# New due times, engine choices and filler share for a scheduled attention and two-MoE kernel

## The chip, the cores and the metric

The kernel runs on one core of a Trainium2 chip. The metric is the device time of one execution in microseconds (us); shorter is better. The engines go by the profile's names: PE (matrix products; PEld is its weight loads), DVE (VectorE), ACT (ScalarE), POOL (GpSimd), and SP, which issues the DMAs.

## What is computed

A gated linear attention over 4 batches, 8 heads, 768 steps and head size 48, and behind it two pairs of dense layers ("MoE") over all 3072 tokens, 384 wide and 2048 deep:

```python
state = alpha[t] * state + k[t] ⊗ v[t]          # per batch and head, 48x48
y[t]  = q[t] @ state
...
h = x @ w_in                                    # first pair
P = a[0] + a[1]*h + a[2]*h*h + a[3]*h*h*h
Q = 1.0 + |b[0]|*|h| + |b[1]|*h*h
x = (P / (Q + 1e-6)) @ w_out
...
h = x @ w_in2                                   # second pair
out = (h * tanh(softplus(h))) @ w_out2
```

All weights come as 64-bit floats, which the kernel takes apart with integer operations.

## The kernel before

The sequence is cut into six blocks c of 128 steps. **An attention unit** is two batches of one block; there are twelve. A unit runs through levels L = 0, 1, 2, 4, 8, 16, 32 (blocks 0 to 2) or 2 to 32 after a diagonal step (blocks 3 to 5). A level is 32 small products on PE (L476, 64 records in the trace), a masked copy of them into the tile AT (L487, L507 on DVE, or L495, L501 on ACT), and on DVE a scaling of the tiles Q and K by products of alpha (L460). The products of alpha are built by a **tree** of six halving multiplications, which runs on DVE or POOL by the string E_TREE (one letter per block; V is DVE, P is POOL, A is ACT). The next level's product on PE reads the scaled Q and K, so PE and DVE take turns within a unit. Behind the levels stand transposes (L537), an outer product (L552), the state's update (tmp, X), and the outputs (L590, L626).

**A step** of a pair is one of 16 slices of 128 hidden columns for one block. On PE it is a hidden product H, nine matmuls of 512 columns (L682), and an output product O, nine more (L731). In pair l=0 the work between H and O is, on ACT, the absolute value u (L697), a scaled copy (L705), B1*u+B0 (L703), a logarithm and an exponential (L710, L714), on POOL one multiplication (L704), and on DVE three polynomial steps (L706, L708, L715). In pair l=1 it is one activation (L719). Both pairs then split the result g into a rounded part gh (L230 on ACT or L232 on DVE) and the rest gl = g - gh (line 223 on DVE or 225 on POOL, by E_GL0 and E_GL1, one letter per block).

The twelve phases (l, c) of 16 steps follow each other as PHASES says: (0,0), (0,1), (1,0), (0,2), (1,1), (0,3), (1,2), (0,4), (1,3), (0,5), (1,4), (1,5). The buffers are few: three PSUM banks for H, four slots of z and p, three of gh and gl. So H can run only some steps ahead of O. Block c+1's attention runs beside phase (0,c), since phase (0,c+1) needs its output; the conversions of the weights (`load_w`, 32 in all) lie beside the first four phases.

**What sets the order:** nothing is scheduled at run time. Every operation is given to `Plan.add` with an engine, an assumed duration and a due time. `Plan.order` then plays the plan through: each engine that is free takes the ready operation with the earliest due time, and the order in which operations start there is the order in which they are written into each engine's queue. On the chip, a queue runs in that order; an instruction whose input is late holds all behind it. Due times come from the tables T_PH, AT_T, Q_A0, Q_V0, Q_CV and some offsets. In `Plan.order`, DVE and POOL operations marked `port` exclude each other. As long as no H has been placed, free PE time before F_END is filled with matmuls of 256 columns that nobody reads (`warm`, L775), as far as F_RATE allows.

## Time and profile before

| | us |
|---|---|
| three runs | 1011.58, 1009.32, 1011.18; median 1011.18 |
| profiled execution, its own time | 1012.22 |
| its span | 1010.4 |
| PE busy | 969.7 |
| DVE busy | 689.3 |
| ACT busy | 603.4 |
| POOL busy | 252.0 |

The profiled execution took 1.04 us more than the median, and 1.8 us of it lie outside the span. PE is in use nearly throughout, but a busy PE is not a PE at its peak: matmuls overlap, and one that waits for its turn is drawn longer. In a stretch without any wait, nine matmuls of 512 columns follow each other in 2.04 us.

### The profile page before, as it was taken

The numbers are of one execution on the slowest core, as the hardware profiler recorded it, in microseconds if no ns is written. First come the engines' busy times: TensorE is split into PE (matmuls) and PEld (weight loads), VectorE is DVE, ScalarE is ACT, GpSimd is POOL, SyncE is SP. The second block draws the span as 40 slices with busy tenths as digits, with TensorE's granted clock in tenths as the row PEclk, the third lists the DMA queues.
The fourth block names the chain that finished last, engine by engine and source line by source line (L and its number), as shares of the span: only waits on it lengthen the run. The fifth ranks groups of instructions, "written<-read, shape, count | busy, mean of one in ns | idle before, by whom it ended". The sixth has DMA issues, their size and how long they took to land.

```text
span 1010.4 us, 24622 instructions
## 1 busy us (share of the span) xinstructions
PE 969.7 (96%) x10460; PEld 783.9 (78%) x10460; DVE 689.3 (68%) x876; ACT 603.4 (60%) x994; POOL 252.0 (25%) x199
## 2 busy tenths in 40 slices
PE   7899897999999999999999899999999999999998
PEld 6776676778878878878877688878788878888886
DVE  4959999899998899845589963389941178621211
ACT  3659887799756599521487652376541288733332
POOL 2115665433301155102134221045223300000000
PEclk8989998999999999999999999999999999999999
DMA  8455656837778878659538378556365555465630
GB/s 338 147 185 188 221 203 222 285 108 245 258 250 291 281 240 268 174 178 306 163 99 296 89 244 277 142 175 234 110 210 159 144 158 153 140 212 143 180 107 32
DMA packets 75469, 198.39 MB, mean 196 GB/s; under 512 B 8160, under 2 KB 34912, under 8 KB 73824
## 3 DMA queue, kind: packets, MB, share of 16 engines
q1 hardware_dynamic: 75360, 196.82, 60.4%
q8 instruction: 82, 1.34, 0.6%
q14 instruction: 27, 0.22, 0.1%
HBM read 165.34 MB, written 31.46 MB: 195 GB/s over the span
## 4 chain that ended last, share of the span: by engine, by line
PE 66%; DVE 12%; ACT 5%; DMA 3%; issue 2%; POOL 0%; SPq 0%; ACTq 0%; POOLq 0%; DVEq 0%
PE bank L731 31%; PE bank L682 29%; PE pair L476 2%; DVE zp L715 2%; DVE qka L460 2%; PE pair L626 1%; DVE zp L706 1%; DVE zp L708 1%; DMA out_dram<-u 1%; DVE AT L507 1%; DVE gg L223 1%; ACT u L697 1%; ACT zp L710 1%; ACT zp L714 1%; ACT zp L703 1%
## 5 line engine op out<-in xcount | busy, mean ns | idle before, releaser
L731 PE MATMUL bank<-gg,wo 128*128 128x512 f32 x1728 | 432.4, 395 | 1.2 <-DVE gg L223 0.6
L731 PEld LDWEIGHTS bank<-gg,wo 128*128 128x128 f32 x1728 | 324.0, 190 | 70.9 <-DVE gg L223 1.7
L682 PE MATMUL bank<-xh,wih 128*128 128x512 f32 x576 | 231.5, 402 | 5.6 <-DVE zp L708 4.3
L682 PE MATMUL bank<-xl,wih 128*128 128x512 f32 x576 | 225.3, 391 | 0.0
L682 PE MATMUL bank<-xh,wl 128*128 128x512 f32 x576 | 225.1, 391 | 0.0
L223 DVE TENSOR_TENSOR gg<-zp,gg 128x512 fp32r<-128x512 f32 x160 | 122.0, 767 | 133.4 <-ACT gg L230 132.5
L704 POOL TENSOR_TENSOR zp<-zp,u 128x512 f32<-128x512 f32 x80 | 124.1, 1554 | 266.5 <-ACT zp L703 266.2
L719 ACT ACTIVATE zp<-bank 128x512 f32<-128x512 f32 x96 | 57.0, 596 | 206.3 <-PE bank L682 205.8
L682 PEld LDWEIGHTS bank<-xh,wih 128*128 128x128 f32 x576 | 108.7, 189 | 32.2 <-DVE zp L708 7.2
L682 PEld LDWEIGHTS bank<-xh,wl 128*128 128x128 f32 x576 | 108.6, 189 | 23.5
L682 PEld LDWEIGHTS bank<-xl,wih 128*128 128x128 f32 x576 | 108.9, 189 | 21.0
L230 ACT CAST gg<-zp 128x512 fp32r<-128x512 f32 x144 | 89.3, 621 | 38.3 <-DVE zp L715 23.9
L476 PEld LDWEIGHTS pair<-qka 48*64 48x64 f32 (+4 forms) x4160 | 60.7, 129 | 40.4 <-issue 11.2
L476 PE MATMUL pair<-qka 48*64 48x32 f32 (+4 forms) x4160 | 68.3, 215 | 17.5 <-ACT AT L501 5.5
L706 DVE SCALAR_TENSOR_TENSOR zp<-zp,sc,bank 128x512 f32<-128x512 f32 x96 | 70.6, 740 | 12.9 <-ACT zp L705 12.6
L710 ACT ACTIVATE zp<-zp,c 128x512 f32<-128x512 f32 x96 | 69.7, 729 | 10.3 <-POOL zp L704 9.8
L715 DVE SCALAR_TENSOR_TENSOR zp<-zp,sc 128x512 f32<-128x512 f32 x80 | 71.6, 901 | 6.0 <-ACT zp L714 4.7
L705 ACT ACTIVATE zp<-bank,sc 128x512 f32<-128x512 f32 x96 | 66.2, 690 | 15.2 <-PE bank L682 10.2
L708 DVE SCALAR_TENSOR_TENSOR zp<-zp,sc,bank 128x512 f32<-128x512 f32 x96 | 70.9, 743 | 4.5 <-ACT u L697 2.8
L697 ACT ACTIVATE u<-bank 128x512 f32<-128x512 f32 x96 | 57.3, 600 | 24.5 <-PE bank L682 18.3
L232 DVE CAST gg<-zp 128x512 fp32r<-128x512 f32 x48 | 22.5, 472 | 66.9 <-ACT zp L719 63.6
L460 DVE TENSOR_TENSOR qka<-qka,qk 128x1024 f32<-128x1024 f32 x44 | 58.7, 1333 | 12.1 <-PE pair L476 8.4
(148 smaller groups left out, 952.3 us busy)
## 6 DMA issues: line engine op xcount, KB each, us to landing
wo<-woD SPq DMA_DIRECT2D x160, 384.0 KB, 3.3
wl<-wlD SPq DMA_DIRECT2D x160, 192.0 KB, 2.8
qka<-in_qka_dram SPq DMA_DIRECT2D x10, 1536.0 KB, 7.7
woD<-wo SPq DMA_DIRECT2D x16, 768.0 KB, 4.8
wlD<-wl SPq DMA_DIRECT2D x16, 384.0 KB, 3.9
raw<-in_w2o_dram SPq DMA_DIRECT2D x8, 768.0 KB, 5.0
...
```

Source lines behind the costliest of these rows:

```text
L223: dve(n, due, reads, writes, lambda: nc.vector.tensor_tensor(**kw()))
L230: act(n, due, reads, writes, lambda: nc.scalar.copy(out=out(), in_=in_()), src="s")
L460: dve(W, now(), [kT[L]], [kQC, kK], lambda: nc.vector.tensor_tensor(out=QK, in0=QK, in1=Tv.unsqueeze(3).to_broadcast([P, 2, m, L]), op=ALU ...
L476: nc.tensor.matmul(bk[j][o:o + m, lo + 32 * g:lo + 32 * (g + 1)].rearrange("p (n l) -> p n l", l=l), lhsT=K[h, e * HC:e * HC + m], rhs=QC[ ...
L682: nc.tensor.matmul(bank[hb], lhsT=w[:, k * P:(k + 1) * P], rhs=x[k], start=(k == 0 and j == 0), stop=(k == KT - 1 and j == 2))
L697: act(NTOK, due, [kh, "tab"], [ku], lambda: nc.scalar.activation(u, h, AF.Abs), table="ln")
L704: pool(NTOK, due, [ku], [kz], lambda: nc.gpsimd.tensor_tensor(out=zs[r], in0=zs[r], in1=u, op=ALU.mult))
L706: dve(NTOK, due, [kh], [kp], lambda: nc.vector.scalar_tensor_tensor(out=ps[r], in0=ps[r], scalar=A2, in1=h, op0=ALU.add, op1=ALU.mult), po ...
L708: dve(NTOK, due, [kh], [kp], lambda: nc.vector.scalar_tensor_tensor(out=ps[r], in0=ps[r], scalar=A1, in1=h, op0=ALU.add, op1=ALU.mult), po ...
L710: act(NTOK, due, [], [kz], lambda: nc.scalar.activation(zs[r], zs[r], AF.Ln, bias=c_1), src="s", ptr=1, table="ln")
L715: dve(NTOK, due, [kw], [kp], lambda: nc.vector.scalar_tensor_tensor(out=ps[r], in0=ps[r], scalar=A0, in1=w(), op0=ALU.add, op1=ALU.mult), ...
L731: nc.tensor.matmul(bank[5 + k], lhsT=wos[b][:, w, k * P:(k + 1) * P], rhs=x[q], start=(f == 0 and j == 0), stop=(f == FT - 1 and j == 2))
```

## The change

Only the numbers and letters that feed the plan, the assumed cost of a POOL operation, and two new forms of the weight conversion change what is built. In the weight conversion (`load_w`), form A makes the low bits by an activation on ACT; the new form B makes them by a shift on DVE. It is used by 2 of the 32 conversions; form C is used by none. The new letter G in R_PSUM and R_MISH, which keeps g in PSUM, is used by no block, so `split_g` and `hidden` build the same operations as before.

```diff
-T0 = 86.664
+T0 = 103.104
-T_PH = (9.277, 6.654, 6.157, 5.496, 14.285, 12.303, 6.406, 21.64, 8.826, 19.033, 5.941, 6.084)
+T_PH = (9.812, 5.897, 4.97, 0.365, 23.477, 6.33, 6.522, 16.525, 12.473, 8.147, 3.464, 4.853)
...
-E_TREE = 'PPPVPP'
-E_QK = 'VVPPVP'
+E_TREE = 'PPVVVP'
+E_QK = 'VVPPPP'
...
-E_GL1 = 'VVVPVV'
+E_GL1 = 'VVVPPP'
...
-E_LW = 'PVPPPVVVVVVVVVVVVVVVVVVVVVVVVVVV'
+E_LW = 'VVPPPVVGVVVVVVVVVVVVVVVVVVVVVVVV'
...
-E_CV = 'ADAAAAAAADDAADADDDDAADDDAADDDADA'
+E_CV = 'ADAAABAAADDAADADDDBAADDDAADDDADA'
...
-E_L32 = 'AV'
-E_KC = ('AA', 'AV')
+E_L32 = 'AA'
+E_KC = ('AA', 'AA')
...
-E_XH = ('AA', 'VA')
-E_DC = 'PV'
+E_XH = ('VA', 'AA')
+E_DC = 'PP'
...
-F_END = 91.927
-F_RATE = 1325.024
+F_END = 268.634
+F_RATE = 1329.217
...
-        plan.add("POOL", 0.15 + (0.0021 if n > 2 * P else 0.00254) * n, due, reads, writes, emit, True)
+        plan.add("POOL", 0.112 + (0.00217 if n == NTOK else 0.00168) * n, due, reads, writes, emit, True)
...
+            if E_CV[nth] in "BC":
+                dve(n, due, [kr], [kz], lambda: nc.vector.tensor_scalar(
+                    out=zt.bitcast(I32), in0=lw, scalar1=29, scalar2=None, op0=ALU.logical_shift_right), fast=True)
...
+            if E_CV[nth] == "A":
+                act(n, due, [kr], [kz], lambda: nc.scalar.activation(
+                    low3, quarters[:, :, 1], AF.Identity, scale=2.0 ** -13, bias=c_f), src="s", ptr=3.6)
```

The other tables (AT_T, Q_A0, Q_V0, Q_CV, LAG, the offsets) get new values in the same manner. In the built program the lines move: L476 becomes L485, L460 L469, L507 L516, L682 L691, L731 L755, L706 L715, L708 L717, L715 L726, L704 L713, L223 L224, L225 L226. PE has the same H, O and attention products in both, and five fillers more (43 against 38). POOL takes over 32 subtractions gl of phases (1,4) and (1,5) from DVE and gives the trees of blocks 2 and 4 to it; of the weights' rounding remainders (E_LW), one goes from PE to DVE and one from DVE to POOL. Two evictions and four small copies of block 0's second unit go from DVE to ACT.

**DVE in phase (0,3)**, the eighth to tenth step. L706, L708 and L715 are the polynomial steps, gg is a subtraction gl; qka and AT belong to an attention unit of block 4. Before:

```order
L708 SCALAR_TENSOR_TENSOR zp_130<-zp_130,sc_67,bank2_123 128x512
L708 SCALAR_TENSOR_TENSOR zp_130<-zp_130,sc_67,bank3_124 128x512
L507 COPY_PREDICATED AT0_140<-cst_65,pair_122 128x256x2
L460 TENSOR_TENSOR qka0_141<-qka0_141 128x2x256x2
L223 TENSOR_TENSOR gg_131<-zp_130,gg_131 128x512
L715 SCALAR_TENSOR_TENSOR zp_130<-zp_130,sc_67 128x512 x2
L706 SCALAR_TENSOR_TENSOR zp_130<-zp_130,sc_67,bank4_125 128x512
L507 COPY_PREDICATED AT0_140<-cst_65,pair_122 128x128x4
L708 SCALAR_TENSOR_TENSOR zp_130<-zp_130,sc_67,bank4_125 128x512
L706 SCALAR_TENSOR_TENSOR zp_130<-zp_130,sc_67,bank2_123 128x512
L708 SCALAR_TENSOR_TENSOR zp_130<-zp_130,sc_67,bank2_123 128x512
L460 TENSOR_TENSOR qka0_141<-qka0_141,qk0_144 128x2x128x4
```

and now:

```order
L715 SCALAR_TENSOR_TENSOR zp_130<-zp_130,sc_67,bank3_124 128x512
L717 SCALAR_TENSOR_TENSOR zp_130<-zp_130,sc_67,bank3_124 128x512
L715 SCALAR_TENSOR_TENSOR zp_130<-zp_130,sc_67,bank4_125 128x512
L224 TENSOR_TENSOR gg_131<-zp_130,gg_131 128x512
L726 SCALAR_TENSOR_TENSOR zp_130<-zp_130,sc_67 128x512
L717 SCALAR_TENSOR_TENSOR zp_130<-zp_130,sc_67,bank4_125 128x512
L715 SCALAR_TENSOR_TENSOR zp_130<-zp_130,sc_67,bank2_123 128x512
L717 SCALAR_TENSOR_TENSOR zp_130<-zp_130,sc_67,bank2_123 128x512
L224 TENSOR_TENSOR gg_131<-zp_130,gg_131 128x512
L726 SCALAR_TENSOR_TENSOR zp_130<-zp_130,sc_67 128x512 x2
L715 SCALAR_TENSOR_TENSOR zp_130<-zp_130,sc_67,bank3_124 128x512
L224 TENSOR_TENSOR gg_131<-zp_130,gg_131 128x512
```

Both units of block 4 stood in this phase before, the second in the middle of these steps; now no attention work stands in these rows. Counted from the first to the last L715 of the phase, seven scalings L460 became three and four masked copies L507 one; they stand after the phase's last step now.

**PE just before the first H.** L652 (now L661) transposes the last output of block 0; pair products with 64x32 and 60x32 are levels of block 1's first unit, L376 and L377 (now L385, L386) parts of weight conversions. Before:

```order
L652 MATMUL bank6_127<-cst_65,u_129 128x128 x3
L652 MATMUL bank7_128<-cst_65,u_129 128x128 x3
L476 MATMUL pair_122<-qka0_141 64x32 x32
L376 MATMUL bank6_127<-f320_101,cst_65 128x384
L377 MATMUL bank6_127<-wih0_0_71,minus_70 128x384
L376 MATMUL bank7_128<-xf_105,cst_65 128x384
L377 MATMUL bank7_128<-wih0_1_72,minus_70 128x384
L476 MATMUL pair_122<-qka0_141 64x32 x32
L376 MATMUL bank6_127<-xf_105,cst_65 128x384
L377 MATMUL bank6_127<-wih0_1_72,minus_70 128x384
L682 MATMUL bank2_123<-xh_107,wih0_0_71 128x512
L682 MATMUL bank2_123<-xl_108,wih0_0_71 128x512
```

and now:

```order
L485 MATMUL pair_122<-qka0_141 64x32 x32
L385 MATMUL bank6_127<-xf_105,cst_65 128x384
L386 MATMUL bank6_127<-wih0_1_72,minus_70 128x384
L385 MATMUL bank7_128<-xf_105,cst_65 128x384
L386 MATMUL bank7_128<-wih0_1_72,minus_70 128x384
L385 MATMUL bank6_127<-xf_105,cst_65 128x384
L386 MATMUL bank6_127<-wo1_92,minus_70 128x384
L485 MATMUL pair_122<-qka0_141 60x32 x32
L385 MATMUL bank7_128<-f320_101,cst_65 128x384
L386 MATMUL bank7_128<-wih0_2_73,minus_70 128x384
L691 MATMUL bank2_123<-xh_107,wih0_0_71 128x512
L691 MATMUL bank2_123<-xl_108,wih0_0_71 128x512
```

Before, two levels of block 1 stood ahead of the first H, both behind that transposition; now there are four, two of them ahead of it and two (the levels 2 and 4) behind it.

**POOL in phase (0,1).** L704 (now L713) is the multiplication of a step; qka and qk are the tree of block 2's first unit, tmp its state. Before:

```order
L704 TENSOR_TENSOR zp_130<-zp_130,u_129 128x512
L225 TENSOR_TENSOR qka0_141<-qka0_141 128x512
L704 TENSOR_TENSOR zp_130<-zp_130,u_129 128x512
L225 TENSOR_TENSOR qk0_144<-qka0_141 128x256
L225 TENSOR_TENSOR qk0_144<-qk0_144 128x128
L704 TENSOR_TENSOR zp_130<-zp_130,u_129 128x512
L225 TENSOR_TENSOR qk0_144<-qk0_144 128x64
L704 TENSOR_TENSOR zp_130<-zp_130,u_129 128x512
L225 TENSOR_TENSOR qk0_144<-qk0_144 128x32
L704 TENSOR_TENSOR zp_130<-zp_130,u_129 128x512
L225 TENSOR_TENSOR qk0_144<-qk0_144 128x16
L225 TENSOR_TENSOR tmp_139<-X00_135,qk0_144 48x768
```

and now:

```order
L226 TENSOR_TENSOR gg_131<-zp_130,gg_131 128x512 x2
L713 TENSOR_TENSOR zp_130<-zp_130,u_129 128x512
L226 TENSOR_TENSOR gg_131<-zp_130,gg_131 128x512
L713 TENSOR_TENSOR zp_130<-zp_130,u_129 128x512
L226 TENSOR_TENSOR gg_131<-zp_130,gg_131 128x512 x2
L226 TENSOR_TENSOR tmp_139<-X00_135,qk0_144 48x768
L713 TENSOR_TENSOR zp_130<-zp_130,u_129 128x512 x6
L226 TENSOR_TENSOR tmp_139<-X00_135,qk0_144 48x768
```

The six operations of the tree are gone from POOL; they stand on DVE. So it is for both units of blocks 2 and 4.

## Rows read from the trace of the kernel before

**Rows 1.** The page: busy time and share; shares of the chain that ended last.

```profile
PE 969.7 (96%) x10460; PEld 783.9 (78%) x10460; DVE 689.3 (68%) x876; ACT 603.4 (60%) x994; POOL 252.0 (25%) x199
...
PE 66%; DVE 12%; ACT 5%; DMA 3%; issue 2%; POOL 0%; SPq 0%; ACTq 0%; POOLq 0%; DVEq 0%
```

**Rows 2.** Stretches: us, busy us by engine (instructions), PE clock, DMA share, GB/s.

```profile
70.90:277.10 206.20, 191.96 (x2598) 152.06 (x2596) 195.27 (x223) 177.65 (x291) 98.12 (x73) 0.98 0.64 217
277.10:340.30 63.20, 61.99 (x749) 50.11 (x748) 54.25 (x69) 36.47 (x56) 4.45 (x2) 1.00 0.81 281
340.30:424.30 84.00, 82.55 (x897) 66.64 (x895) 75.64 (x102) 68.47 (x116) 32.09 (x20) 1.00 0.73 229
424.30:492.60 68.30, 68.16 (x726) 55.56 (x719) 35.88 (x51) 15.48 (x28) 7.21 (x8) 1.00 0.70 223
492.60:592.00 99.40, 94.03 (x1231) 74.68 (x1230) 85.29 (x98) 73.85 (x126) 34.37 (x25) 0.97 0.54 163
592.00:652.40 60.40, 60.26 (x443) 49.69 (x442) 22.67 (x28) 20.69 (x35) 8.05 (x8) 1.00 0.73 238
652.40:740.00 87.60, 85.73 (x1204) 68.05 (x1203) 79.31 (x106) 57.64 (x96) 31.42 (x23) 1.00 0.54 167
...
806.80:1010.40 203.60, 198.38 (x874) 163.64 (x873) 83.86 (x122) 104.00 (x176) 1.28 (x1) 1.00 0.48 140
```

**Rows 3.** Groups by line: busy us, mean ns; idle before them, releaser.

```profile
L476 PE MATMUL pair<-qka 48*64 48x32 f32 (+4 forms) x4160 | 68.3, 215 | 17.5 <-ACT AT L501 5.5 <-issue 3.6 <-DVE AT L507 3.3
...
L460 DVE TENSOR_TENSOR qka<-qka,qk 128x1024 f32<-128x1024 f32 x44 | 58.7, 1333 | 12.1 <-PE pair L476 8.4 <-issue 3.7
...
L507 DVE COPY_PREDICATED AT<-cst,pair 128x512 f32<-128x512 int32 x35 | 31.5, 900 | 3.9 <-PE pair L476 3.8
```

**Rows 4.** Groups by line: the tree of alpha on POOL and on DVE.

```profile
L225 POOL TENSOR_TENSOR qk<-qk 128x128 f32<-128x128 f32 (+4 forms) x40 | 28.7, 716 | 15.9 <-DMA qk<-in_nat_dram 13.9
...
L225 POOL TENSOR_TENSOR qka<-qka 128x512 f32<-128x512 f32 x9 | 11.7, 1298 | 66.6 <-DVE qka L447 66.6
...
L225 POOL TENSOR_TENSOR qk<-qka 128x256 f32<-128x256 f32 x9 | 10.2, 1132 | 0.5
...
L223 DVE TENSOR_TENSOR qk<-qk 128x128 f32<-128x128 f32 (+4 forms) x10 | 3.8, 384 | 4.7 <-DMA qk<-in_nat_dram 4.5
...
L223 DVE TENSOR_TENSOR qka<-qka 128x512 f32<-128x512 f32 x2 | 1.8, 908 | 0.0
...
L223 DVE TENSOR_TENSOR qk<-qka 128x256 f32<-128x256 f32 x2 | 1.2, 602 | 0.0
```

**Rows 5.** PE in order of time, first H: start, us, what, idle before.

```profile
44.04 1.13 PE L775 MATMUL bank<-cst 128*128 128x256 f32 x4
...
61.96 0.82 PE L652 MATMUL bank<-cst,u 128*128 128x128 f32 x6
...
70.92 0.40 PE L682 MATMUL bank<-xh,wih 128*128 128x512 f32 x1
...
76.93 1.08 PE L476 MATMUL pair<-qka 48*60 48x32 f32 x64 [0.36 <-DVE AT L507]
...
80.91 1.03 PE L476 MATMUL pair<-qka 48*56 48x32 f32 x64
```

**Rows 6.** DVE in order of time, in phase (0,3).

```profile
565.61 2.19 DVE L460 TENSOR_TENSOR qka<-qka,qk 128x1024 f32<-128x1024 f32 x1
...
571.88 1.21 DVE L460 TENSOR_TENSOR qka<-qka,qk 128x1024 f32<-128x1024 f32 x1
```

**Rows 7.** POOL in order of time, in phase (0,3).

```profile
565.44 1.27 POOL L704 TENSOR_TENSOR zp<-zp,u 128x512 f32<-128x512 f32 x1 [3.67 <-ACT zp L703]
```

**Rows 8.** PE in order of time, in phase (0,3).

```profile
567.86 1.65 PE L476 MATMUL pair<-qka 48*56 48x32 f32 x64 [1.88 <-DVE qka L460]
```

**Rows 9.** Groups by line: the subtraction gl on DVE and on POOL.

```profile
L223 DVE TENSOR_TENSOR gg<-zp,gg 128x512 fp32r<-128x512 f32 x160 | 122.0, 767 | 133.4 <-ACT gg L230 132.5
...
L225 POOL TENSOR_TENSOR gg<-zp,gg 128x512 fp32r<-128x512 f32 x32 | 43.4, 1355 | 69.6 <-DVE gg L232 46.1 <-ACT gg L230 19.6 <-issue 3.9
```

More of the change, by code (lines that the diff above doesn't have):

```diff
@@ L710, in hidden @@
             act(NTOK, due, [], [kz], lambda: nc.scalar.activation(zs[r], zs[r], AF.Ln, bias=c_1), src="s", ptr=1, table="ln")
-            kw = kh if R_PSUM[c] == "R" else kz
-            w = lambda: h if R_PSUM[c] == "R" else zs[r]
+            kw = kh if R_PSUM[c] in "RG" else kz
+            w = lambda: h if R_PSUM[c] in "RG" else zs[r]
+            ko = kh if R_PSUM[c] == "G" else kp
+            o = lambda: h if R_PSUM[c] == "G" else ps[r]
             act(NTOK, due, [kz], [kw] + (["tab"] if last else []),
@@ L714, in hidden @@
                 lambda: nc.scalar.activation(w(), zs[r], AF.Exp, scale=-1.0), src="s", table="ln")
-            dve(NTOK, due, [kw], [kp], lambda: nc.vector.scalar_tensor_tensor(
-                out=ps[r], in0=ps[r], scalar=A0, in1=w(), op0=ALU.add, op1=ALU.mult), port=R_PSUM[c] != "R", ptr=1)
-        else:
-            act(NTOK, due, [kh] + ([] if last else ["tab"]), [kp] + (["tab"] if last else []),
-                lambda: nc.scalar.activation(ps[r], h, AF.Mish), table="mish")
-    def split_g(l, r, q, i, due):
+            dve(NTOK, due, [kw, kp], [ko], lambda: nc.vector.scalar_tensor_tensor(
+                out=o(), in0=ps[r], scalar=A0, in1=w(), op0=ALU.add, op1=ALU.mult), port=R_PSUM[c] not in "RG", ptr=1)
+        else:
+            ko, o = (kh, h) if R_MISH[c] == "G" else (kp, ps[r])
+            act(NTOK, due, [kh] + ([] if last else ["tab"]), [ko] + (["tab"] if last else []),
+                lambda: nc.scalar.activation(o, h, AF.Mish), table="mish")
@@ L722, in split_g @@
+    def split_g(l, r, q, hb, i, due):
         c = steps[i][1]
-        kp, kgh, kgl = f"p{r}", f"gh{q}", f"gl{q}"
-        copy(E_GH[l][c], NTOK, due, [kp], [kgh], lambda: ghs[q], lambda: ps[r])
-        tt((E_GL0, E_GL1)[l][c], NTOK, due, [kp, kgh], [kgl],
-           lambda: dict(out=gls[q], in0=ps[r], in1=ghs[q].bitcast(F32), op=ALU.subtract))
+        in_bank = (R_PSUM, R_MISH)[l][c] == "G"
+        kp, kgh, kgl = f"bank{hb}" if in_bank else f"p{r}", f"gh{q}", f"gl{q}"
+        g = bank[hb] if in_bank else ps[r]
+        eng = E_GH[l][c]
+        if in_bank and eng == "A":
+            act(NTOK, due, [kp], [kgh], lambda: nc.scalar.copy(out=ghs[q], in_=g))
+        elif in_bank:
+            dve(NTOK, due, [kp], [kgh], lambda: nc.vector.tensor_copy(out=ghs[q], in_=g), port=False)
+        else:
+            copy(eng, NTOK, due, [kp], [kgh], lambda: ghs[q], lambda: g)
+        if in_bank:
+            dve(NTOK, due, [kp, kgh], [kgl], lambda: nc.vector.tensor_tensor(
+                out=gls[q], in0=g, in1=ghs[q].bitcast(F32), op=ALU.subtract), port=False)
+        else:
+            tt((E_GL0, E_GL1)[l][c], NTOK, due, [kp, kgh], [kgl],
+               lambda: dict(out=gls[q], in0=g, in1=ghs[q].bitcast(F32), op=ALU.subtract))
@@ L819, in attention_moe_kernel @@
         hidden(l, hb, r, i, V[i] + D_MID)
-        split_g(l, r, q, i, V[i] + D_MID + D_SPL[l])
+        split_g(l, r, q, hb, i, V[i] + D_MID + D_SPL[l])
         out_mms(f, q, b, V[i] + LAG[l])
```

37 lines of the change are left out of this document (20 added, 17 removed).

## Prediction, made before the changed kernel was run

> **What bounds the kernel now.** I read the page first, then the stretches, then the groups, then single instructions. The page [rows 1] has PE busy 96% of the span and two thirds of the chain that ended last on PE, with 12% on DVE: a PE kernel that waits for DVE at places. Where it waits, the stretches tell [rows 2], one for each phase or two. I take PEld, not PE, as the measure, since a waiting matmul is drawn longer while a weight load isn't. In phase (1,1) (424.3 to 492.6) PE is busy 68.16 of 68.30 us and PEld 55.56, a share of 0.813 with attention among the products. That is a stretch nearly without waits, and its share tells how long the others would take without any:
>
> - (0,0) and (0,1), 206.20 us: 152.06 / 0.813 = 187.0, so at most 19.2 can be won
> - (1,0), 63.20 us: 50.11 / 0.813 = 61.6, at most 1.6
> - (0,2), 84.00 us: 66.64 / 0.813 = 82.0, at most 2.0
> - (0,3), 99.40 us: 74.68 / 0.813 = 91.9, at most 7.5
> - (0,4), 87.60 us: 68.05 / 0.813 = 83.7, at most 3.9
>
> Together 34 us, and the first 70.92 us before the first H [rows 5] beside them. The last stretch, from 806.8, has 874 matmuls, nearly all of 512 columns at 2.04/9 = 0.227 us, so 198 of its 203.6 us: nothing to win but the tail. In the first two phases DVE is busy 195.27 of 206.20 us (95%), in (0,3) 85.29 of 99.40: there DVE sets the pace. In (1,1) and (1,2) it is busy 35.88 of 68.30 and 22.67 of 60.40: there it has room. So what matters of a new order is where it puts DVE's work.
>
> **Part 1, up to the first H.** PE now has two more levels of block 1 ahead of the first H, both behind the transposition that ended a little after 61.96 [rows 5]. A level costs PE 1.03 to 1.08 us, but the next one needs DVE in between: in the old trace the levels at 76.93 and 80.91 follow each other by 3.98 us. If both links lie bare ahead of the first H, it comes 2 x 3.98 = 8.0 us later. If the unit has begun earlier (two levels stand ahead of that transposition now, where none stood), they cost nothing. I take 2 us, nearer to zero, since the first H waited behind PE's queue and weight parts anyway for 70.92 - 61.96 = 9 us. The fillers are five more; two of them (four records) took 1.13 us [rows 5], so five are 2.8 us. They stand where PE waits for a level: 0, at most 2.8 if no wait covers them. Bounds of the part: -1 to +8.
>
> **Part 2, phases (0,0) and (0,1).** I took every DVE instruction of both orders at the mean of its group in the view by line and summed up to the last polynomial step L715 of (0,1). The new order has 5.2 us less DVE work up to there: two conversions less (they come later), two scalings less at 1.333 us [rows 3], but a tree more. A tree costs POOL 1.298 + 1.132 + 4 x 0.716 = 5.3 us and DVE 0.908 + 0.602 + 4 x 0.384 = 3.0 us [rows 4]. While DVE is the pace, 5.2 us less work is 5.2 us less time. I take -4, since the extra levels of part 1 are in that sum already and ACT, busy 177.65 of 206.20 us, has no less to do. Bounds 0 to -8 (the tree no longer on POOL may free DVE by another 3).
>
> **Part 3, (1,0) and (0,2).** What was put off arrives: up to the first L715 of (0,2) the sum is 3.4 us above the old one, so 8.6 us of DVE work more fall between. In (1,0) DVE was idle for 63.20 - 54.25 = 8.95 us, so it just fits: 0 to +5, I take +1.5. In (0,2) 10.8 us of DVE work go away, the diagonal step of block 3's second unit among them, and come back in (1,1), where DVE was idle for 32 us. The limit is the 2.0 us above; I take -1.5.
>
> **Part 4, (0,3).** Both units of block 4 ran in this phase, on PE the first from its 2nd H on and the second from its 13th. In the new order five of the nine levels are left in it, and the second unit runs in (1,2). DVE's work between the phase's first and last L715 falls by 14.0 us of 70.0: four L460 at 1.333 and three L507 at 0.900 are 8.0 [rows 3], the rest is five single operations and one L708 that slid out. The cover is (1,2), where DVE was idle for 37.7 us. How PE waits in (0,3) is to be seen at 567.86: 1.88 us idle until DVE's scaling had ended [rows 8], which itself took 2.19 us instead of the 1.21 of its neighbour [rows 6], beside an L704 on POOL [rows 7]. Without the second unit such waits go, and 7.5 us is the most that PE can give back. What is late next is the step itself: ACT, busy 73.85 us of 99.40. I take -5; bounds -7.5 and 0.
>
> **Part 5, the rest.** Block 5's second unit moves some seven PE products later, out of (0,4) towards (1,3): I take -1 of the 3.9. The 32 subtractions that go to POOL take 1.355 instead of 0.767 us [rows 9], but between a step's H and its O stand several products of 2.04 us, and nothing else is on POOL there; at the very end the last gl comes 0.6 us later, while three O of the steps before still run. Cost 0, at most +0.6. The new conversions, evictions and remainders are in the DVE sums. PE's clock, 0.97 to 1.00 in these stretches, moves with the waits: (0,3) has 0.97 of it, and I leave that in the 7.5.
>
> **The sum:** +2 - 4 + 1.5 - 1.5 - 5 - 1 = -8. The profiled execution took 1012.22 us and its span 1010.4; with -8 it is 1004.2, and its like in the measure of the median (1011.18, 1.04 less) is **1003 us**, 0.8% faster.
>
> **Rivals.** *The levels bunch up (slower).* In the new order of PE, 21 levels follow the one before with only one H or O, 2.04 us, between (19 with one or none in the old), four of them in a row in (0,1), where DVE is full. All waits before L476 in the old trace are 17.5 us on PE [rows 3]. If the wait of 1.88 us [rows 8] falls on half of those 21 anew, it is 20 us more, and the sum is -8 + 20 = +12: 1023 us; it turns the sign at some six such waits. For it speaks that the queue is rigid; against, that the levels moved go to phases with idle DVE, and that the old order with nearly as many has those 17.5 only. A smaller form ends near 1016.
>
> *What is put off is paid later (no change).* The 8.6 us of part 3 don't fit into the 8.95, and the first H comes the full 8 us late: -8 + 3.5 + 6 = +1.5, some 1012.5. For it: up to the last l=0 step the new order has 3.8 us more DVE work in all. Against: part 4 doesn't depend on it.
>
> *POOL holds DVE for its whole length (faster still).* The scaling at 565.61 took 0.98 us longer than its neighbour, and POOL's L704 ran for 1.10 us of it [rows 6, 7]. If all of a tree's 5.3 us held DVE in this manner, three trees that leave POOL in phases where DVE sets the pace free 16 us against the 9 us that DVE takes over and that the sums hold already: 1003 - 16 = 987 us. Against it speaks the mean of the 44 scalings, 1.333 us [rows 3]: 0.12 above 1.21, so 5 us in the whole kernel.
>
> The Trainium skill, page "SBUF — State Buffer", section "Who interferes with whom", states this rule: a VectorE operation with two inputs in SBUF and a GpSimd operation that reads SBUF exclude each other, and the later one blocks fully. The trace agrees at 565.61 (0.98 us lost of an overlap of 1.10). By the rule taken for every tree, the sum would be the third rival's; by the mean row it is mine. The rule also speaks against the change at one place, the one remainder that goes to POOL in (0,0).
>
> **How the numbers follow.** A measurement of this kernel can tell some 0.2%, 2 us, from no change, so faster is below 1009.2 and slower above 1013.2. The forecast has 0.56, of which 0.02 gain too little to be told; the levels that bunch up 0.20, of which 0.18 end above 1013.2 and 0.02 within; the work paid later 0.16, half of it within, a quarter on either side; full holding by POOL 0.08. Faster: 0.54 + 0.04 + 0.08 = 0.66. Within 0.2%: 0.02 + 0.02 + 0.08 = 0.12. Slower: 0.18 + 0.04 = 0.22. The range is 990 to 1016: its low end leaves out most of the third rival, its high end the worse half of the first.
>
> **What would show it.** Right: the first H between 70 and 75 us; the last O of (0,1) some 2 us earlier than 277; PE without waits above 1 us in the stretch of (0,3), that stretch near 94 us, and (1,2) still at 60 to 61. Wrong: the first H after 77 us; idle before L476 above 27 us; (1,0) longer than 67 us; a wait of PE in (1,2), which had none.

## The result, and the profile after

The changed kernel takes 997.46 us (median of 4 runs, 996.72 to 1000.23) beside 1011.09 (4 runs, 1009.32 to 1011.58): a ratio of 0.9873, 95% interval 0.9851 to 0.9896, 1.3% faster. A second set of six runs gave 998.4 us and 0.987 (0.9851 to 0.989). The forecast was 1003, faster, with a range of 990 to 1016: sign and range held, the gain is 13.6 us where 8 were forecast. The profiled execution took 1000.23 us with a span of 998.4; against 1012.22 and 1010.4 that is 12.0.

The page of the changed kernel, busy time and chain, answers to [rows 1]. VectorE is busy 40 us less (689.3 before), GpSimd 20 us more, and PE's share of the chain is 74% instead of 66, DVE's 4% instead of 12 (79% and 10% in a second profiled execution of the same kernel, so DVE's fall there is not firm):

```profile
PE 964.8 (97%) x10464; PEld 783.4 (78%) x10464; DVE 649.1 (65%) x862; ACT 600.2 (60%) x997; POOL 271.7 (27%) x211
...
PE 74%; ACT 5%; DVE 4%; DMA 1%; issue 1%; SPq 0%; ACTq 0%; DVEq 0%
```

To see where the time went, I cut both traces at the same products: the start, then at the first H of (0,0), (1,0), (0,2), (0,3), (0,4) and (0,5). Columns as in [rows 2]. The kernel before:

```profile
0.00:70.90 70.90, 59.85 (x1463) 48.14 (x1464) 44.90 (x60) 33.25 (x47) 14.45 (x23) 0.86 0.62 223
70.90:250.00 179.10, 164.86 (x2361) 129.89 (x2360) 169.50 (x193) 155.07 (x259) 89.21 (x64) 0.97 0.62 209
250.00:340.30 90.30, 89.09 (x985) 72.28 (x984) 80.02 (x99) 59.04 (x89) 13.36 (x11) 1.00 0.79 277
340.30:492.60 152.30, 150.71 (x1615) 122.20 (x1614) 111.52 (x152) 83.95 (x144) 39.30 (x28) 1.00 0.72 226
492.60:652.40 159.80, 154.29 (x1672) 124.37 (x1671) 107.96 (x125) 94.54 (x160) 42.42 (x33) 0.98 0.61 191
652.40:806.80 154.40, 152.53 (x1498) 123.39 (x1497) 91.53 (x130) 73.52 (x121) 52.03 (x39) 1.00 0.57 172
```

and the changed one, with the last stretch to the end, which is 203.60 us in both [rows 2]:

```profile
0.00:81.30 81.30, 64.64 (x1605) 51.68 (x1606) 51.84 (x64) 37.94 (x56) 17.25 (x25) 0.90 0.57 209
81.30:252.80 171.50, 162.69 (x2232) 129.56 (x2231) 150.59 (x188) 147.40 (x249) 81.46 (x58) 0.96 0.63 214
252.80:343.60 90.80, 89.67 (x1047) 72.74 (x1046) 85.05 (x113) 62.54 (x94) 10.31 (x6) 1.00 0.79 272
343.60:493.80 150.20, 148.93 (x1608) 121.11 (x1607) 110.63 (x153) 83.08 (x144) 34.40 (x22) 1.00 0.72 229
493.80:640.90 147.10, 146.85 (x1599) 119.34 (x1598) 99.55 (x128) 92.64 (x160) 36.47 (x28) 1.00 0.65 205
640.90:794.80 153.90, 153.65 (x1514) 125.40 (x1507) 90.47 (x131) 73.75 (x121) 49.39 (x39) 1.00 0.58 175
794.80:998.40 203.60, 198.37 (x874) 163.59 (x873) 60.97 (x90) 102.88 (x176) 42.47 (x33) 1.00 0.47 140
```

The differences are +10.4, -7.6, +0.5, -2.1, **-12.7**, -0.5 and 0. Up to the first H of (0,3) nothing is gained (492.6 and 493.8 us; 490.7 in a second execution); the whole gain stands in (0,3) and (1,2). Part of it is only where the cut falls: PE has 73 instructions fewer in that stretch, a product O of nine (2.04 us) and a level (1.05 us), 3.1 us of work that stands in its neighbours. The other 9.6 us are waits and a slower clock that are gone. The view of PE's waits of the changed kernel has no row at all from 493.8 to 640.9; that of the kernel before, from 492 to 653, has (what PE waits for: us in total, times, longest):

```profile
PE pair L476 <- DVE qka L460: 2.5, 2, 1.9
PE pair L476 <- ACT AT L501: 2.1, 1, 2.1
PE bank L682 <- DVE zp L708: 0.5, 2, 0.3
PE bank L731 <- DVE gg L223: 0.2, 1, 0.2
```

### The profile page after: what moved, and what is told of

The parts are those of the page before. It is cut to its first block, busy times and chain, and to the rows that moved or that the text cites. A ratio compares the mean times of both kernels' runs of the same rounds, so it can differ in the third digit from the quotient of the medians.

```text
span 998.4 us, 24631 instructions
## 1 busy us (share of the span) xinstructions
PE 964.8 (97%) x10464; PEld 783.4 (78%) x10464; DVE 649.1 (65%) x862; ACT 600.2 (60%) x997; POOL 271.7 (27%) x211
## 4 chain that ended last, share of the span: by engine, by line
PE 74%; ACT 5%; DVE 4%; DMA 1%; issue 1%; SPq 0%; ACTq 0%; DVEq 0%
PE bank L755 35%; PE bank L691 33%; PE pair L485 3%; PE pair L635 2%; DVE qka L469 1%; PE pair L546 1%; PE pair L561 1%; DMA raw<-in_w2o_dram 1%; DMA raw<-in_w2i_dram 1%; ACT zp L719 1%; ACT gg L231 1%; DVE AT L516 1%; ACT zp L712 1%; ACT f L352 1%; ACT u L706 0%
## 5 line engine op out<-in xcount | busy, mean ns | idle before, releaser
L755 PE MATMUL bank<-gg,wo 128*128 128x512 f32 x1728 | 426.9, 393 | 0.6 <-ACT u L768 0.5
L755 PEld LDWEIGHTS bank<-gg,wo 128*128 128x128 f32 x1728 | 320.5, 188 | 68.0 <-ACT u L768 0.6
L691 PE MATMUL bank<-xh,wih 128*128 128x512 f32 x576 | 230.3, 400 | 5.5 <-DVE zp L726 3.7
L691 PE MATMUL bank<-xh,wl 128*128 128x512 f32 x576 | 225.8, 392 | 0.0
L691 PE MATMUL bank<-xl,wih 128*128 128x512 f32 x576 | 225.6, 392 | 0.0
L713 POOL TENSOR_TENSOR zp<-zp,u 128x512 f32<-128x512 f32 x80 | 115.5, 1446 | 230.4 <-ACT zp L712 230.0
L731 ACT ACTIVATE zp<-bank 128x512 f32<-128x512 f32 x96 | 57.0, 596 | 147.5 <-PE bank L691 108.4
L226 POOL TENSOR_TENSOR gg<-zp,gg 128x512 fp32r<-128x512 f32 x64 | 85.4, 1336 | 220.5 <-ACT gg L231 163.5
L231 ACT CAST gg<-zp 128x512 fp32r<-128x512 f32 x144 | 89.1, 622 | 80.0 <-PE bank L755 75.0
L691 PEld LDWEIGHTS bank<-xh,wih 128*128 128x128 f32 x576 | 108.8, 189 | 30.8 <-DVE zp L726 4.7
L691 PEld LDWEIGHTS bank<-xh,wl 128*128 128x128 f32 x576 | 108.8, 189 | 23.3
L691 PEld LDWEIGHTS bank<-xl,wih 128*128 128x128 f32 x576 | 108.9, 189 | 21.4
L224 DVE TENSOR_TENSOR gg<-zp,gg 128x512 fp32r<-128x512 f32 x128 | 96.2, 755 | 38.2 <-ACT gg L231 37.6
L715 DVE SCALAR_TENSOR_TENSOR zp<-zp,sc,bank 128x512 f32<-128x512 f32 x96 | 71.0, 743 | 23.0 <-ACT zp L714 22.0
L485 PEld LDWEIGHTS pair<-qka 48*64 48x64 f32 (+4 forms) x4160 | 60.3, 129 | 31.4 <-DVE AT L516 13.1
L226 POOL TENSOR_TENSOR tmp<-X,qk 48x768 f32<-48x768 f32 x19 | 29.9, 1572 | 176.9 <-DVE X L575 87.0
L719 ACT ACTIVATE zp<-zp,c 128x512 f32<-128x512 f32 x96 | 69.6, 729 | 10.4 <-POOL zp L713 9.8
L485 PE MATMUL pair<-qka 48*64 48x32 f32 (+4 forms) x4160 | 67.8, 215 | 8.2 <-DVE AT L516 6.7
L714 ACT ACTIVATE zp<-bank,sc 128x512 f32<-128x512 f32 x96 | 66.3, 691 | 12.9 <-PE bank L691 12.6
L717 DVE SCALAR_TENSOR_TENSOR zp<-zp,sc,bank 128x512 f32<-128x512 f32 x96 | 71.2, 744 | 4.2 <-ACT u L706 2.5
L726 DVE SCALAR_TENSOR_TENSOR zp<-zp,sc 128x512 f32<-128x512 f32 x80 | 63.4, 796 | 8.5 <-ACT zp L725 7.5
L766 DVE COPY u<-bank 128x512 f32<-128x512 f32 x12 | 8.3, 692 | 93.2 <-PE bank L755 93.1
```

What stands on the lines that cost most here:

```text
L224: dve(n, due, reads, writes, lambda: nc.vector.tensor_tensor(**kw()))
L226: pool(n, due, reads, writes, lambda: nc.gpsimd.tensor_tensor(**kw()))
L231: act(n, due, reads, writes, lambda: nc.scalar.copy(out=out(), in_=in_()), src="s")
L485: nc.tensor.matmul(bk[j][o:o + m, lo + 32 * g:lo + 32 * (g + 1)].rearrange("p (n l) -> p n l", l=l), lhsT=K[h, e * HC:e * HC + m], rhs=QC[ ...
L691: nc.tensor.matmul(bank[hb], lhsT=w[:, k * P:(k + 1) * P], rhs=x[k], start=(k == 0 and j == 0), stop=(k == KT - 1 and j == 2))
L713: pool(NTOK, due, [ku], [kz], lambda: nc.gpsimd.tensor_tensor(out=zs[r], in0=zs[r], in1=u, op=ALU.mult))
```

## The experiments

**Block 4's units, there and back.** The move on which part 4 rests, undone and made by block 4's due times alone. In the changed kernel:

```diff
-AT_T = (..., (-11.632, 15.427, 158.362), ...)
+AT_T = (..., (0.72, 25.86, 54.77), ...)
```

> The changed kernel with one number triple altered: the due times of block 4 put both of its units into phase (0,3) again (PE then has the second unit's nine levels between the 92nd H and the 91st O, as the kernel before had them). Everything ahead of (0,3) keeps its order. Theory (the gain of the change is the second unit's move out of a phase that DVE fills): (0,3) and (1,2) together, 147.1 us in the changed kernel and 159.8 before, go back to 156 to 160 us, and the time to 1006 to 1011 us. Rival (the gain of these two phases comes from what else was changed: trees off GpSimd, evictions, the order of the conversions): they stay within 2 us of 147, and the time at 996 to 1000 us.

Measured: 1004.28 us (7 runs), ratio to the kernel before 0.994 (0.9919 to 0.9961). And in the kernel before:

```diff
-AT_T = (..., (1.398, 50.331, 106.585), ...)
+AT_T = (..., (-11.632, 25.0, 240.0), ...)
```

> The kernel before with one number triple altered: block 4's second unit is due later, so that PE has its levels between the 98th H and the 99th O, in phase (1,2), as in the changed kernel. Theory (the move alone makes the gain): (0,3) and (1,2) together fall from 159.8 us to 147 to 151, the time from 1011 to 999 to 1003 us. Prediction's cap (7.5 us is all that PE can give back there): 1004 us or more. Rival (the move needs the other edits): within 2 us of 1011.

Measured: 1003.36 us (6 runs), ratio 0.9918 (0.9904 to 0.9932). The stretch of (0,3) and (1,2), columns as above, first of the kernel with the units put back, then, in its own fence, of the kernel before with the units moved:

```profile
492.20:645.00 152.80, 147.64 (x1599) 119.12 (x1597) 101.06 (x128) 93.23 (x160) 43.29 (x28) 1.00 0.62 197
```

```profile
491.90:643.80 151.90, 150.81 (x1673) 121.92 (x1672) 101.21 (x125) 93.81 (x160) 39.20 (x33) 1.00 0.64 201
```

Made alone, the move takes 7.9 us off the 159.8, with the same products in the stretch; undone alone, it puts 5.7 back on the 147.1. So it carries most of the 9.6 us, and neither theory had it whole: of the change's 13 to 14 us it makes 6 to 8, the other edits the rest (the kernel with the units put back is still 7 us faster than before). With the 3.1 us of work on the other side of the cut counted, these others make 2 to 4 us in this stretch, and 2.5 in (0,4) and (1,3), where half a microsecond less holds one product more.

A triple holds a block's first due time, the distance to its second unit, and the length over which a unit's steps are due, so both edits move the first unit too. On PE its outputs stand behind the 8th H of (0,3) in the kernel before, the 9th with the units put back, the 14th with them moved, and the 17th in the changed kernel; the second unit's first level with a product on PE stands behind the 13th, 13th, 18th and 20th, the last two of them in (1,2). So these runs show what block 4's new places are worth, both units together; what the second unit's move makes of it by itself is not shown.

How the move helps is in VectorE's column. The kernel before and the one with the units moved have the same 125 VectorE instructions in this stretch, and they take 107.96 and 101.21 us. The groups tell which (line, engine, names, shapes, count | busy, mean ns | idle before). The kernel before:

```profile
L223 DVE TENSOR_TENSOR gg<-zp,gg 128x512 fp32r<-128x512 f32 x32 | 27.5, 868 | 35.4 <-ACT gg L230 35.3
L715 DVE SCALAR_TENSOR_TENSOR zp<-zp,sc 128x512 f32<-128x512 f32 x16 | 16.9, 1064 | 2.0 <-ACT zp L714 1.9
L708 DVE SCALAR_TENSOR_TENSOR zp<-zp,sc,bank 128x512 f32<-128x512 f32 x16 | 11.8, 742 | 0.3
...
L704 POOL TENSOR_TENSOR zp<-zp,u 128x512 f32<-128x512 f32 x16 | 24.4, 1526 | 73.3 <-ACT zp L703 73.2
```

With the units moved:

```profile
L223 DVE TENSOR_TENSOR gg<-zp,gg 128x512 fp32r<-128x512 f32 x32 | 22.5, 709 | 28.6 <-ACT gg L230 28.5
L715 DVE SCALAR_TENSOR_TENSOR zp<-zp,sc 128x512 f32<-128x512 f32 x16 | 13.5, 849 | 2.2 <-ACT zp L714 2.2
L708 DVE SCALAR_TENSOR_TENSOR zp<-zp,sc,bank 128x512 f32<-128x512 f32 x16 | 11.9, 744 | 0.3
...
L704 POOL TENSOR_TENSOR zp<-zp,u 128x512 f32<-128x512 f32 x16 | 23.1, 1446 | 58.8 <-ACT zp L703 58.7
```

And the changed kernel (L726 is L715 of before, L717 is L708, L713 is L704):

```profile
L726 DVE SCALAR_TENSOR_TENSOR zp<-zp,sc 128x512 f32<-128x512 f32 x16 | 12.0, 755 | 1.7 <-ACT zp L725 1.6
L717 DVE SCALAR_TENSOR_TENSOR zp<-zp,sc,bank 128x512 f32<-128x512 f32 x16 | 11.8, 744 | 0.3
...
L713 POOL TENSOR_TENSOR zp<-zp,u 128x512 f32<-128x512 f32 x16 | 22.2, 1391 | 52.8 <-ACT zp L712 52.7
```

The polynomial step that reads both inputs from SBUF takes 1064, 849 and 755 ns; its sister with one input in PSUM, of the same size, takes 742 to 744 in all three. GpSimd's multiplication gets shorter along with it, 1526, 1446 and 1391. Single instructions tell why. Of the 80 steps L715 of the kernel before, 52 ran beside no GpSimd operation and took 733 to 753 ns; 28 overlapped one and took 735 to 1959, 1188 on average. L708 took 742 ns beside none and 743 beside one (48 each). So VectorE and GpSimd hold each other up, on VectorE operations with two inputs in SBUF, and the order decides how often. The Trainium skill, page "SBUF — State Buffer", section "Who interferes with whom", says just this: a VectorE instruction with two SBUF inputs contends with a GpSimd instruction that reads SBUF, one with at most one SBUF input, outside the two-port modes, doesn't. The trace agrees on both halves: 1188 against 746 ns for the first, 743 against 742 for the second.

**The trees back on GpSimd.** The changed kernel in its own order, with the trees of blocks 2 and 4 issued on the other engine:

```diff
-    tt(E_TREE[c], ..., op=ALU.mult))
+    tt(E_TREE[c], ..., op=ALU.mult), "P" if c in (2, 4) else None)   # the plan keeps E_TREE
```

> The changed kernel in its own order, with the four trees of alpha of blocks 2 and 4 issued on GpSimd instead of VectorE (24 instructions; VectorE has 4 x 3.0 = 12 us less work, GpSimd 4 x 5.3 = 21 us more). Theory A (each engine's own time counts): phases that VectorE paces get shorter, 992 to 997 us. Theory B (GpSimd's two-input work holds VectorE for its whole length): VectorE loses 5.3 where it saves 3.0 us a tree, 2.3 us a tree, so 999 to 1007 us. If neither sets the pace where trees stand: within 2 us of 997.5.

Measured: 996.75 us (6 runs, 992.73 to 1002.1), beside 998.4 (995.76 to 1000.41) of the changed kernel: no difference, as the third forecast had it. Its page, and under it that of the second profiled execution of the changed kernel, show why (line 1):

```profile
PE 962.9 (97%) x10464; PEld 781.1 (78%) x10464; DVE 645.1 (65%) x838; ACT 599.9 (60%) x997; POOL 297.1 (30%) x235
```

```profile
PE 960.5 (96%) x10464; PEld 779.5 (78%) x10464; DVE 647.7 (65%) x862; ACT 599.9 (60%) x997; POOL 273.3 (27%) x211
```

In the changed kernel the six trees of blocks 2 to 4 take VectorE 4.1 + 3.6 + 5.3 = 13.0 us (6 at 689 ns, 6 at 606, 24 at 220), so four take 8.7. VectorE's busy time falls by 2.6 only, or by 4.0 against the 649.1 of the first profiled execution: some 24 us more of GpSimd cost VectorE's other work 4.7 to 6.1 us. Theory B's price, a hold for the whole length, would be all 24; a fifth to a quarter of GpSimd's time is what it cost here. The choice of engine for the trees is worth nothing by itself.

**The subtractions gl back on VectorE.**

```diff
-    tt((E_GL0, E_GL1)[l][c], ..., op=ALU.subtract))
+    tt((E_GL0, E_GL1)[l][c], ..., op=ALU.subtract), "V" if l == 1 and c > 3 else None)
```

> The changed kernel in its own order, with the 32 subtractions gl of phases (1,4) and (1,5) issued on VectorE instead of GpSimd. The prediction gave this part 0 to 0.6 us: expected 996.5 to 998 us, the stretch of the last three phases at 203.6 us. Rival (it costs or brings something that the stretch hides, such as a later last product): more than 2 us either way.

Measured: 996.93 us (6 runs), the last stretch 203.6 us as before (from 793.4 to the end at 997.0), while VectorE is busy 670.9 us instead of 647.7. So 23 of the 40 us by which VectorE is less busy are these, and they bring nothing: part 5's 0 holds.

**More work for VectorE.** If VectorE sets a stretch's pace, work added to it must show. The subtraction gl was issued twice, with the same inputs and output, in the 16 steps of one phase:

```diff
-    lambda: nc.vector.tensor_tensor(**kw())
+    lambda: [nc.vector.tensor_tensor(**kw()) for _ in range(2 if (l, c) == (0, 1) else 1)]
```

> The changed kernel with the subtraction gl issued twice in each of the 16 steps of (0,1): 16 x 0.796 = 12.7 us more work for VectorE there, and nothing else altered. If VectorE's work alone sets the pace of (0,0) and (0,1), as the prediction has it, the stretch from the first H to the first H of (1,0), 168.7 to 171.5 us in the changed kernel, gets 10 to 13 us longer and the time is 1008 to 1011 us. If VectorE has room by now (it is busy 69.96 of 81.60 us from the first H of (0,1) to that of (1,0)): at most 4 us, 997 to 1002 us.

> The changed kernel with gl issued twice in each of the 16 steps of (0,3), 12.7 us more for VectorE. With the second unit gone from it, VectorE is busy 48.58 of 61.90 us in the stretch of its H products, so by the theory the 13.3 us of room take it up: (0,3) and (1,2) together stay at 147 to 150 us, the time at 997 to 1001. Rival (VectorE sets the pace there still): 157 to 160 us, the time 1007 to 1011.

> The same 16 subtractions doubled in (0,3) of the kernel before, where VectorE is busy 75.88 of 86.70 us and has both units of block 4. By the theory it is the bound there: (0,3) and (1,2) together go from 159.8 to 166 to 173 us, the time from 1011 to 1017 to 1024. Rival (what was slow there was the place of single waits and of the clock, not VectorE's sum of work): within 3 us of 159.8, the time within 3 of 1011.

Measured in (0,1) of the changed kernel: 1010.54 us (10 runs) against 998.4, +12.1. VectorE itself is busy 17.2 us more (664.9 against 647.7), not 12.7, since the doubled operations meet GpSimd too. In the profiled execution, the fastest of the ten (1007.79), 7.4 us of the loss stand before the first H of (1,0) (176.1 us instead of 168.7, less than the 10 to 13 expected there) and 4.7 behind it (96.2 instead of 91.5). So most of the work added in (0,1) shows as time, as it would if VectorE had next to no room there. A doubled subtraction also lengthens each step's way from H to O by itself; this run can't tell that from the sum of VectorE's work.

In (0,3) of the changed kernel the stretch is 156.6 us instead of 147.1, +9.5, in the profiled execution; that one is the slowest of its four (1008.45; median 1003.78, so +5.4 by medians). In (0,3) of the kernel before it is 166.1 instead of 159.8, +6.3 (1018.51 us against 1012.5), as forecast. But it should have cost nothing in the changed kernel, and there my theory for (0,3) fell: the 13.3 us that VectorE is idle are not free room. The stretch of the changed kernel with the doubled work:

```profile
492.60:649.20 156.60, 148.80 (x1600) 118.79 (x1598) 116.69 (x144) 93.33 (x160) 37.61 (x28) 1.00 0.61 192
```

VectorE is busy 17.1 us more (116.69 against 99.55) for 12.7 us added; PE waits 5.3 us for L717 and 1.6 for L224. VectorE's idle time in this stretch was waiting, not room: in the changed kernel 21.7 us of it stand ahead of L224, nearly all for ACT's L231. That what is added in between delays what is queued behind is my reading; no run separates it.

**The start.** Four runs on why the first H comes so late. The changed kernel once more, as their measure:

> The changed kernel once more, beside the three edits of its start that run with it. Expected: a median of 995 to 1000 us; the first H at 80 to 83 us, the first H of (1,0) at 249 to 253, and the 147.1 us of (0,3) and (1,2) again to 0.2.

Measured: 998.4 us, the first H at 80.1 us, that of (1,0) at 248.8, and 147.1 us again. PE around the end of block 0 in the first profiled execution (start, us, what, idle before), to be laid beside [rows 5], where the same transposition L652 stands at 61.96. `bank<-zp` is a level of block 0's second unit, `bank<-X,qka` begins the first unit's outputs; in the kernel before, the last such level stands ahead of these outputs:

```profile
45.10 1.36 PE L476 MATMUL bank<-zp 48*32 48x32 f32 x64
46.40 0.96 PE L590 MATMUL bank<-X,qka 48*64 48x48 f32 x26
```

and in the changed kernel the last two stand behind them:

```profile
44.17 0.96 PE L599 MATMUL bank<-X,qka 48*64 48x48 f32 x26
...
49.69 1.55 PE L485 MATMUL bank<-zp 48*48 48x32 f32 x62
...
55.49 0.76 PE L485 MATMUL bank<-zp 48*32 48x32 f32 x64
...
58.49 1.07 PE L546 MATMUL bank<-cst,zp 128*128 128x128 f32 x8
...
59.92 1.14 PE L485 MATMUL pair<-qka 48*64 48x32 f32 x64
...
63.91 0.74 PE L561 MATMUL bank<-u,zp 64*48 64x48 f32 x45 [2.59 <-issue]
...
66.00 1.93 PE L485 MATMUL pair<-qka 48*64 48x32 f32 x64
...
71.66 2.93 PE L799 MATMUL bank<-cst 128*128 128x256 f32 x6
74.38 1.29 PE L661 MATMUL bank<-cst,u 128*128 128x128 f32 x6
...
81.28 0.39 PE L691 MATMUL bank<-xh,wih 128*128 128x512 f32 x1
```

From the transposition to the first H it is 6.9 us, less than the 9.0 of before; the transposition itself comes 12.4 us later. The first unit's outputs begin 2.2 us earlier than before. From them to the transposition it is 30.2 us here (28.3 to 30.2 in seven executions with this order and these fillers), and 15.6 in the kernel before. The last level of block 0's second unit stands at 55.49, and in its tail stand two levels of block 1, one at half clock (1.2 GHz) for 1.93 us, a stall of 2.59 us at issue, and fillers, the last of 2.93.

```diff
-AT_T = (..., (-46.773, 23.453, 116.65), ...)
+AT_T = (..., (-20.0, 23.453, 116.65), ...)
```

> The changed kernel with block 1's first unit due later, so that two of its levels go from ahead of the first H to behind it. The order up to the last transposition of block 0 stays. The prediction's reason (the two levels are what delays the first H, 4 us each when bare): first H 4 to 8 us earlier, at 73 to 77 us. Rival (the delay is in block 0's own second unit, whose chain ends at 74 to 75 us instead of 62): first H at most 3 us earlier, at 78 or later. In both cases the two levels come back in (0,0), where VectorE sets the pace: the first H of (1,0) within 3 us of 251, the time 994 to 1001 us.

Measured: 1002.55 us (0.991, 0.9893 to 0.9927), 4 us slower than the changed kernel. Ahead of the first H the trace has one level fewer (1541 PE instructions instead of 1605), not two. The first H comes at 82.3, no earlier, but this execution is 5 us late before the edit can tell: the first unit's outputs begin at 49.25 instead of 44.06, with a mean granted clock of 0.86 up to them instead of 1.00, though all engines run the same instructions in the same order up to there. From these outputs to the transposition (76.90) it is 27.7 us, nearly as long as the 28.3 to 30.2 of the changed kernel; from there to the first H it is 5.4 instead of 6.4 to 7.5, so a level costs 1 to 2 us there, and the delay lies ahead of the transposition. The rival holds. The loss comes later: the first H of (1,0) at 250.3 is in time, and up to that of (0,2) it is 95.5 us instead of 91.5, with a level and a product more in that stretch.

The numbers of the kernel before for the start (block 0's due times, those of loads and conversions, T0, and the engines of these). The conversions lie beside the first four phases, so this edit reaches further than the start:

> The changed kernel with the kernel before's numbers for the start alone (due times and engines of block 0, of the weight loads and conversions, and the due time of the first phase). First H back at 70 to 75 us. Theory (the late start was given back because VectorE sets the pace of (0,0) and (0,1), whichever product of PE comes first): the first H of (1,0) stays at 248 to 252 us and the time at 994 to 999. Rival (the late start cost what it shows, and something else made the gain behind it): the first H of (1,0) comes 6 to 10 us earlier, at 241 to 245, and the time is 987 to 992 us.

Block 0's second unit due earlier:

```diff
-AT_T = ((-15.582, -16.399, -37.503), ...)
+AT_T = ((-15.582, -55.0, -37.503), ...)
```

> The changed kernel with block 0's second unit due 39 us earlier, so that PE has all of its levels ahead of both units' outputs (they stood behind the first unit's outputs and a stall of 2.9 us there) and block 1 begins with two levels fewer ahead of the first H. If that queue is what delays the start: first H at 70 to 76 us. What it is worth by the end follows the same two theories as the start of before: 994 to 999 us where VectorE sets the pace, 987 to 992 where it doesn't.

Measured: 1011.66 us (0.9998, 0.9982 to 1.0014) and 1020.25 (1.0085, 1.0067 to 1.0104). Both have the transposition early (68.2 and 67.3 us) and the first H earlier (76.9 and 78.3), and both lose it and more by the first H of (1,0): 260.6 and 257.1 us instead of 248.8. No theory had that. The stretch between of the two:

```profile
76.90:260.60 183.70, 168.54 (x2367) 132.76 (x2366) 167.05 (x201) 158.87 (x265) 86.00 (x60) 0.95 0.65 215
```

```profile
78.30:257.10 178.80, 163.00 (x2345) 129.61 (x2345) 153.31 (x191) 148.52 (x249) 83.33 (x58) 0.94 0.62 205
```

The first has 201 VectorE instructions there and 167.05 us of them, where the changed kernel has 188 and 150.47, and VectorE is busy 91% of the stretch. Of these 16.6 us more, 4.4 are work that the changed kernel does ahead of the first H (51.16 us there against 46.80). The rest is operations that the changed kernel does only behind the first H of (1,0), eleven by count, and operations that take longer. The second has nearly the changed kernel's VectorE work (191 and 153.31) and waits for it: PE 4.8 us for L575, 3.8 for L516, and 4.0 for ACT's L504. What in its order makes these waits stays open. What both show is that the numbers hang together: a start that is earlier by itself, put under due times that were set for another, loses 13 and 22 us.

Last, the ten fillers behind the first outputs of block 0 left out (products whose result nobody reads):

```diff
     def warm():
+        warmed.append(1)
+        if len(warmed) > 33:
+            return
```

> The changed kernel without the last 10 of its 43 filler products, those behind the first outputs of block 0 (the ones from 52.5 us on; 7.7 us of PE there, much of it at half clock). If they stand in the way of block 0's second unit: the first H comes 3 to 6 us earlier than 80 to 81. If they only fill waits: within 1.5 us. If the clock falls without them: later. VectorE's pace decides what is left of it at the first H of (1,0): within 2 us of 251, and the time at 995 to 1000.

Measured: 998.7 us, no difference. The first H comes at 84.6, but the missing fillers are not what made it late. The first unit's outputs, ahead of the first filler left out, begin at 51.10 instead of 44.06: up to there all engines run the same instructions in the same order, and this execution had a lower clock for another reason. Its start, cut at these outputs, and the stretch behind the first H; then the same of the changed kernel:

```profile
0.00:51.10 51.10, 41.54 (x906) 32.53 (x906) 27.71 (x34) 19.74 (x28) 9.51 (x17) 0.80 0.54 196
51.10:84.60 33.50, 27.38 (x679) 21.50 (x679) 24.40 (x31) 18.04 (x29) 6.97 (x9) 0.69 0.58 209
84.60:252.60 168.00, 157.50 (x2234) 124.83 (x2233) 152.23 (x188) 147.08 (x249) 81.85 (x58) 1.00 0.65 218
```

```profile
0.00:44.10 44.10, 33.30 (x908) 26.41 (x908) 27.58 (x34) 19.94 (x28) 10.40 (x17) 1.00 0.63 228
44.10:80.10 36.00, 29.74 (x700) 23.84 (x700) 23.58 (x31) 18.03 (x29) 7.71 (x9) 0.81 0.54 193
80.10:248.80 168.70, 159.70 (x2232) 127.12 (x2232) 150.47 (x188) 147.03 (x249) 81.76 (x58) 0.98 0.65 217
```

From the outputs to the first H it takes 33.5 us without the ten fillers, and 34.7 to 37.3 in the seven executions with the changed kernel's order and all of them. The transposition comes 24.4 us behind the outputs instead of 28.3 to 30.2, and from it to the first H it takes 9.2 instead of 6.4 to 7.5, at a lower clock: 0.69 from the outputs on instead of 0.81, and the weight parts L385 and L386 at 78.38 take 1.64 and 1.09 us instead of 0.91 and 0.63. So with the ten fillers the end of block 0 comes 4 to 6 us later, and the higher clock behind it gives some 2 of them back, in the one execution that was profiled. The kernel's time shows none of it. No version tried is faster than the changed kernel by more than runs of one kernel differ.

## Why the prediction was right, and where it was not

**Part 1, the start (+2, bounds -1 to +8; measured +10.4): wrong in place, and outside its bounds.** It priced two added levels as standing behind the last transposition. Two stood behind it before, and two do now; a level is cheap there, as it took (1 to 2 us, by the run with the level behind). The two that the order adds stand ahead of that transposition, and "they cost nothing" was said of exactly those. What it left out is that they and the fillers stand in the tail of block 0's second unit, whose own last levels went behind the first unit's outputs: the transposition comes 12.4 us later. The fillers, put at 0, hold it up by 4 to 6 of these by the run without them. The sign "wrong if the first H comes after 77 us" was met, at 81.3.

**Part 2 (-4; measured -7.6): within its bounds, its reason only in part.** The last O of (0,1) comes at 275.8 us (271.8 in the second execution), where 2 us before 277 was the sign. But "5.2 us less work is 5.2 us less time" does not describe what happened. By the means of the groups before, VectorE's work up to the last polynomial step of (0,1) was to fall by 5.2 us; the durations of its instructions up to there fell by 15.5 (247.3 to 231.8), since the same operations are held up less. In the stretch itself VectorE is busy 18.9 us less (169.50 to 150.59), and the time fell by 7.6, some of which is the two levels that moved into the start. VectorE was nearer to setting this stretch's pace before than it is now (95% and 88% busy), though work added to it still shows as time for the most part. The price of a tree was read from a group that mixes the tree with a multiplication of 128x768: by shape, one costs POOL 4.5 us, not 5.3, and DVE 2.4, not 3.0.

**Part 3 (+1.5 and -1.5; measured +0.5 and -2.1): right in size.** Parts 1 to 3 summed to -2 at the first H of (0,3); measured +1.2 in this execution, and -1.9 in the second one of the changed kernel (490.7 us). So the late start was given back. It is not that a late start costs nothing: with the order kept, the stretch behind it took 167.1 to 171.5 us in seven executions, whether the first H came at 80.1 or at 84.6. The start is longer, and this stretch shorter, in part because 6.9 us more of VectorE's work (51.84 against 44.90) and two levels stand in the start and are missing behind it.

**Part 4 (-5, bounds -7.5 to 0; measured -12.7 for (0,3) and (1,2), 9.6 of it waits and clock): mechanism right, two sizes off.** Block 4's move, of both its units, is worth 5.7 to 7.9 us. Cut at the same O, the last but one of (0,3), the phase takes 85.1 us instead of 98.9 (493.8 to 578.9; 94 was forecast), and the rest to the first H of (0,4) 62.0 instead of 60.9. The first size is the cap. I took PEld as a measure that waits don't stretch; but the clock does. The kernel before and that with the units moved have the same loads in this stretch, 124.37 us with a clock of 0.98 and 121.92 with 1.00. By the prediction's 0.813, the stretch without any wait is 121.92 / 0.813 = 150.0, not 153.0, and 9.8 us could be won, not 6.8. The second is VectorE's hold. I worked out 0.12 us for each of 44 scalings, 5 us in all, and let that stand for all its work. For the scalings it was right, and they were the wrong sample. An estimate from the single instructions, what those beside a GpSimd operation took above the mean of those beside none: 12.4 us for the polynomial step on SBUF, 12.6 for gl and 5.1 for the scalings, 30 together in the kernel before, and 4.1 + 8.8 + 3.0 = 16 in the changed one. So VectorE is held 14 us less in these three alone, for the larger part through the order: the trees back on GpSimd took VectorE's other work 4.7 to 6.1 us and no time. The rival that GpSimd holds VectorE is a part of what happened; how much of the 13.6 us it makes is not shown by itself.

**Part 5 (-1 for (0,4), 0 for gl): right.** (0,4) and (1,3) took 0.5 us less with one product more, so 2.5 less in waits, within the 3.9 of the cap; the last stretch is unchanged, and gl put back on VectorE changes nothing.

**The other rivals.** The levels don't bunch up: all waits ahead of them fell from 17.5 to 8.2 us (the idle time ahead of L485), where more than 27 was its sign. What was put off is not paid later: up to the last stretch, no stretch behind the start is more than 0.5 us longer. The view of PE's waits names none in (1,2), as forecast.

The sum came out near because errors cancelled: 8.4 us too little loss in the start, 5.2 too little gain behind it up to (0,3), 7.7 too little in (0,3) and (1,2), of which 3.1 is the place of the cut. Two of the parts lie outside their own bounds, so that the sum is near is partly luck.
